# Second MLP product of an attention and MLP kernel: 512 columns of each tile in a PSUM bank of its own, the remaining 128 of all tiles in a fifth bank, finished first

## The chip, the core and the metric

The kernel runs on one core of one Trainium2 chip. The metric is the time of one execution on the device, in microseconds (us); the median of several executions is compared. The core's engines are named as in the profile: PE (TensorE, matrix products into PSUM), PEld (its weight loads), DVE (VectorE), ACT (ScalarE), POOL (GpSimd) and SP (SyncE, which issues most DMAs). All of them run their own instruction streams in order and wait for each other by semaphores.

## What is computed

Two rounds of a sliding-window attention layer and an MLP, on 2048 tokens of 640 channels, in float32:

```python
x = A_x
x = x + attention(layernorm(x), A_wqkv, A_wo)      # 32 heads of 20, 8 keys at distance 2
x = x + mlp(layernorm(x), B_w1, B_b1, B_w2, B_b2)
x = x + attention(layernorm(x), A_wqkv, A_wo)
x = x + mlp(layernorm(x), B_w1, B_b1, B_w2, B_b2)

def mlp(x, w1, b1, w2, b2):
    y = layernorm(x)
    h = gelu(y @ w1 + b1)          # 640 -> 1536
    return h @ w2 + b2             # 1536 -> 640: the second MLP product
```

## The kernel before

**Units and rounds.** The tokens are cut into four units of 512 tokens (four tiles of 128), and there are two rounds, so eight unit-rounds `n` = 0 to 7. Each goes through the product for q, k and v (`qkv`, matmuls at L513), the windowed attention, which is nearly all DVE work (`attention`, L580 to L627), the output product (`project`, matmuls at L646, 120 for a unit, fed by four DMA transposes of `ohl` that SP issues at L635), a layernorm (`layernorm`, L444 to L489) and the MLP (`mlp`, L661). The rounds of different units overlap: while DVE works on the attention of one unit, PE runs the MLP of an earlier one.

**Precision.** Each float32 operand is split into a high and a low float16 half, and a product is three passes (`PASS`, L497): high by high, high by low, low by high. The low half of the hidden values is made on DVE (L694) from the one that ACT makes (L692).

**The MLP.** `PARTS` (L41) gives nine parts: the first unit-round in two parts of two tiles (P0 and P1 here), the others in parts of four tiles (P2 to P8). Each part goes over 12 slices `e` of 128 hidden channels. For each slice PE makes the first product (`inner`, 15 matmuls at L683 into one of three `ps` banks), ACT applies gelu, and PE then adds the slice's share of the second product (`outer`, L699; matmuls at L707) into the tile `accs`, which holds 2560 float32 columns, that is five PSUM banks of 512. Tile `i` of a part holds the columns from `i * 640` to `(i + 1) * 640`, so `outer` cuts it at the bank edges: 512 + 128 columns for tile 0, 384 + 256 for tile 1, 256 + 384 for tile 2, 128 + 512 for tile 3. A slice of a four-tile part is 24 matmuls: four tiles, three passes, two cuts each; in P0 and P1 it is 12. The sums stay in `accs` over all 12 slices. In the last slice, when a tile is finished, DVE adds its 640 columns to the residual stream `xf` (`residual`, L718 to L720), and in the second round SP stores the tile (L725).

**What sets the order.** The order on each engine is not that of the loops. Every step is handed to a planner (`Plan`, L49) with an estimated duration, a priority, what it needs, what it gives and which buffers (`use`) it takes. The planner runs a model of the engines and then emits all steps in the order in which the model starts them. DVE steps with a priority below -200 may start up to `PATIENCE` (L63) late in the model and still be preferred. Each of the five banks of `accs` is a buffer `acc0` to `acc4` that a part takes and gives back. The waits between engines are not made by the planner: a layer below it adds them, from the tiles that each instruction reads and writes, in the order in which they are emitted. `accs` is one tile.

Of the kernel before, what the change touches and what calls it, by code (L numbers as in the profile page):

```python
# [11 lines left out]
OP = mybir.AluOpType  # L12
AX = mybir.AxisListType

S, D, H, DH, W, DIL, F = 2048, 640, 32, 20, 8, 2, 1536
P = 128
KD = D // P
NF = F // P
# [4 lines left out]
WS = 64.0  # L23
EPS = 1e-5
BANK = 512


UNITS = ((0, 0, 4), (0, 512, 4), (1, 0, 4), (1, 512, 4))
NU = len(UNITS)
M = 4  # L30
# [18 lines left out]
class Plan:  # L49
# [10 lines left out]
    REACH = 1.2  # L60
    LAND = 1.0

    PATIENCE = 0.7  # L63
    ORDERED = ("qk", "v", "yT", "o", "ohl", "c1", "c2", "hh", "h32", "ev")

    def __init__(self, slots):
# [9 lines left out]
    def add(self, eng, dur, prio, emit, need=(), give=(), use=(), table=None, move=0.0, lazy=False):  # L76
        o = dict(eng=eng, dur=dur, prio=prio, emit=emit, need=need, give=give, use=use, table=table,
                 move=move, lazy=lazy, n=len(self.ops))
        self.ops.append(o)
        for u in use:  # L80
            if u not in self.users and u[0] in self.ORDERED and u not in self.line.setdefault(u[0], []):
                self.line[u[0]].append(u)
            self.users[u] = self.users.get(u, 0) + 1
# [107 lines left out]
def sliding_dilated_then_mlp_kernel(  # L191
# [60 lines left out]
    def tile_of(pool, key):  # L252
        return T[pool][plan.slot[pool, key]]
# [31 lines left out]
    def dve(n, prio, emit, need=(), give=(), use=(), more=0.0):  # L285
        plan.add("dve", v_cost(n) + more, prio, emit, need, give, use)
# [11 lines left out]
    def mm(cols, n, prio, emit, need=(), give=(), use=()):  # L298
        plan.add("pe", cols / 2400.0 + 0.0028 * n, prio, emit, need, give, use)
# [117 lines left out]
    def layernorm(n, prio, yk, twice):  # L417
# [25 lines left out]
        for t in range(0 if fast else m):  # L443
            act(D, prio, lambda t=t: nc.scalar.activation(junk, x[u][:, t], AF.Copy, scale=-1.0 / D,  # L444
                                                          accum_out=col(0)[:, t:t + 1]),
                need=[("xh", n, t, 0), ("xh", n, t, 1)] if twice else [("x", la, u, t)], give=[("mn", name, t)],
                use=[lk], acc=1)
            act(D, prio, lambda t=t: nc.scalar.activation(junk, x[u][:, t], AF.Square, bias=col(0)[:, t:t + 1],
                                                          accum_out=col(1)[:, t:t + 1]),
                need=[("mn", name, t)], give=[("sq", name, t)], use=[lk], acc=1, ptr=1)  # L450
# [210 lines left out]
    def mlp(at, b, t0, t1):  # L661

        la, u = divmod(b, NU)
        nt = (t1 - t0) * P
        yk = ("yT", ("b", b))
        ready = [("yT", ("b", b), t) for t in range(t0, t1)]

        def banks(i):
            return [(f"acc{k}", at) for k in range(i * D // BANK, ((i + 1) * D - 1) // BANK + 1)]

        for e in range(NF):
            j = at * NF + e
            pk, hk, h32 = ("ps", ("in", j)), ("hh", j), ("h32", j)
            ck, wk = ("c1", j), ("c2", j)
            for i, k in enumerate((ck, wk)):
                dma(328, -250 + j + 1.5 * i, lambda k=k, i=i, e=e: nc.sync.dma_start(tile_of(*k), mw[i][e]),
                    need=[("mw", e, i)], give=[k], use=[k])

            def inner(ck=ck, pk=pk):
                i = 0  # L680
                for k in range(KD):
                    for a, c in PASS:
                        nc.tensor.matmul(tile_of(*pk)[:, :nt], tile_of(*ck)[:, a, k * P:(k + 1) * P],  # L683
                                         transposed(yk)[:, c * KD + k, t0 * P:t1 * P], start=i == 0, stop=i == 3 * KD - 1)
                        i += 1

            mm(3 * KD * nt, 15, j - 1.0 - AHEAD, inner, need=[*ready, ck, *split_done] + [("hhi", j - 2)] * (e > 1), give=[("hp", j)],
               use=[yk, ck, pk])
            act(nt, -430, lambda pk=pk, h32=h32, e=e: nc.scalar.activation(  # L689
                tile_of(*h32)[:, :nt], tile_of(*pk)[:, :nt], AF.Gelu_apprx_tanh, bias=b1[:, e:e + 1], scale=1.0 / WS),  # L690
                need=[("hp", j), "b1"], give=[("h", j)], use=[pk, h32], table="gelu", ptr=1)
            act(nt, -440, lambda h32=h32, hk=hk: nc.scalar.activation(tile_of(*hk)[:, 0, :nt], tile_of(*h32)[:, :nt], AF.Copy),  # L692
                need=[("h", j)], give=[("hhi", j)], use=[h32, hk])
            dve(nt, -1000, lambda h32=h32, hk=hk: nc.vector.tensor_sub(  # L694
                tile_of(*hk)[:, 1, :nt], tile_of(*h32)[:, :nt], tile_of(*hk)[:, 0, :nt]),
                need=[("hhi", j)], give=[("hlo", j)], use=[h32, hk])
            seen = set()

            def outer(i, passes, wk=wk, hk=hk, e=e, seen=seen):  # L699
                cuts = [i * D]  # L700
                while cuts[-1] < (i + 1) * D:
                    cuts.append(min((i + 1) * D, (cuts[-1] // BANK + 1) * BANK))
                for a, c in passes:
                    for c0, c1 in zip(cuts, cuts[1:]):
                        first = e == 0 and c0 // BANK not in seen
                        seen.add(c0 // BANK)
                        nc.tensor.matmul(accs[:, c0:c1], tile_of(*hk)[:, a, (i - t0) * P:(i - t0 + 1) * P],  # L707
                                         tile_of(*wk)[:, c, c0 - i * D:c1 - i * D], start=first,
                                         stop=e == NF - 1 and (a, c) == PASS[-1], skip_group_check=True)

            for i in range(t0, t1):
                prev = [("out", b, e - 1, i)] if e else ([("outh", b, e, i - 1)] if i > t0 else [])
                mm(2 * D, 4, j, lambda i=i, outer=outer: outer(i, PASS[:2]), need=[("hhi", j), wk, *prev],
                   give=[("outh", b, e, i)], use=[wk, hk, *banks(i)])
                mm(D, 2, j - 0.1, lambda i=i, outer=outer: outer(i, PASS[2:]), need=[("hlo", j), ("outh", b, e, i)],
                   give=[("out", b, e, i)], use=[wk, hk, *banks(i)])
        for i in range(t0, t1):
            def residual(i=i):  # L718
                xt = x[u][:, i]
                nc.vector.scalar_tensor_tensor(xt, accs[:, i * D:(i + 1) * D], 1.0 / WS, xt, op0=OP.mult, op1=OP.add)  # L720

            dve(D, -990, residual, need=[("out", b, NF - 1, i), ("xb", b, i)], give=[("x", la + 1, u, i)],
                use=banks(i))
            if la == 1:
                dma(328, -900, lambda i=i: nc.sync.dma_start(rows(out, u)[:, i], x[u][:, i]),  # L725
                    need=[("x", la + 1, u, i)], give=[("done", u, i)])


    load_x(0, -1000)
# [59 lines left out]
```

## Time and profile before

| | us |
|---|---|
| Median of three runs | 1186.52 (1186.27 to 1188.34) |
| The profiled execution | 1188.67 |
| Its span, first to last instruction | 1186.7 |
| PE busy | 1152.7 (97%) |
| DVE busy | 1015.5 (86%) |
| ACT busy | 511.2 (43%) |

An instruction's busy time on PE overlaps the next one's, since matmuls are pipelined: what a matmul costs is the distance from its start to the next one's. The idle time of a group is the time for which its engine stood still just before it, with the instruction that ended the wait. In the timeline, a row can hold several like instructions in succession; its shape is that of the first. Where nothing else is said, times in the trace count from the start of the span.

### The profile page before, as it was taken

The numbers are of one execution on the slowest core, as the hardware profiler recorded it, in microseconds if no ns is written. First come the engines' busy times: TensorE is split into PE (matmuls) and PEld (weight loads), VectorE is DVE, ScalarE is ACT, GpSimd is POOL, SyncE is SP. The second block draws the span as 40 slices with busy tenths as digits, with TensorE's granted clock in tenths as the row PEclk, the third lists the DMA queues.
The fourth block names the chain that finished last, engine by engine and source line by source line (L and its number), as shares of the span: only waits on it lengthen the run. The fifth ranks groups of instructions, "written<-read, shape, count | busy, mean of one in ns | idle before, by whom it ended". The sixth has DMA issues, their size and how long they took to land.

```text
span 1186.7 us, 17119 instructions
## 1 busy us (share of the span) xinstructions
PE 1152.7 (97%) x6844; PEld 643.8 (54%) x6844; DVE 1015.5 (86%) x979; ACT 511.2 (43%) x921; POOL 54.9 (5%) x46
## 2 busy tenths in 40 slices
PE   5999999999999999999999999999999999999997
PEld 2444446577555465445655465556455655565554
DVE  6999999999999999899999999999999999721211
ACT  5476433545265335632626254364333433352111
POOL 1001001100000000200000010010100000000000
PEclk9999999999999999999999999999999999999999
DMA  9999999778876568557556658575856764544431
GB/s 299 278 331 250 306 337 297 226 255 263 210 196 210 177 157 206 163 167 229 133 182 190 196 135 212 172 206 161 191 185 197 186 212 131 138 110 126 137 100 67
DMA packets 219628, 234.99 MB, mean 198 GB/s; under 512 B 129868, under 2 KB 170140, under 8 KB 219548
## 3 DMA queue, kind: packets, MB, share of 16 engines
q1 hardware_dynamic: 190492, 194.57, 58.2%
q10 hardware_dynamic: 29056, 39.33, 10.0%
q8 instruction: 53, 0.87, 0.3%
q14 instruction: 27, 0.22, 0.1%
HBM read 158.93 MB, written 44.78 MB: 172 GB/s over the span
## 4 chain that ended last, share of the span: by engine, by line
PE 88%; DVE 6%; DMA 3%; issue 1%; ACT 1%; POOL 1%; SPq 0%; DVEq 0%; ACTq 0%
PE ps L513 31%; PE accs L707 24%; PE ps L683 23%; PE ps L646 10%; DVE xf L720 1%; DVE pr L580 1%; DVE sm L584 1%; DMA yT<-hl 1%; POOL ln L461 1%; DVE pr L606 1%; DVE pr L614 1%; DMA qk<-spill 1%; DMA c<-mw 1%; DMA pr<-in_A_wqkv_dram 0%; ACT hl L478 0%
## 5 line engine op out<-in xcount | busy, mean ns | idle before, releaser
L513 PE MATMUL ps<-wq,yT 128*128 128x480 f16 x1920 | 392.8, 367 | 2.0 <-DVE wq L344 1.1
L707 PE MATMUL accs<-c,act 128*128 128x512 f16 (+3 forms) x2304 | 333.0, 299 | 16.6 <-DVE xf L720 12.8
L683 PE MATMUL ps<-yT,c 128*128 128x512 f16 (+1 forms) x1620 | 328.2, 356 | 0.6 <-DMA yT<-hl 0.5
L513 PEld LDWEIGHTS <-yT 128*128 128x128 f16 x1920 | 188.0, 98 | 203.7 <-issue 4.7
L707 PEld LDWEIGHTS <-act 128*128 128x128 f16 x2304 | 204.9, 98 | 139.2 <-issue 18.1
L683 PEld LDWEIGHTS <-c 128*128 128x128 f16 x1620 | 158.1, 98 | 146.0 <-issue 0.8
L689 ACT ACTIVATE act<-ps,b 128x512 f32<-128x512 f32 (+1 forms) x108 | 68.9, 638 | 296.0 <-PE ps L683 285.8
L580 DVE TENSOR_TENSOR pr<-qk 128x2560 f32<-128x2560 f32 x64 | 179.2, 2802 | 1.9 <-DMA qk<-spill 1.8
L584 DVE TENSOR_REDUCE sm<-pr 128x128 f32<-128x2560 f32 x64 | 179.5, 2805 | 0.0
L606 DVE TENSOR_TENSOR pr<-sm,v 128x2560 f32<-128x2560 f32 x64 | 179.0, 2817 | 0.1
L694 DVE TENSOR_TENSOR act<-act 128x512 f16<-128x512 f32 (+1 forms) x108 | 67.7, 628 | 102.9 <-ACT act L692 102.2
L519 ACT ACTIVATE ev<-ps 128x480 f32<-128x480 f32 x128 | 72.3, 566 | 168.1 <-PE ps L513 163.2
L614 DVE TENSOR_TENSOR pr<-pr 128x640 f32<-128x640 f32 (+1 forms) x128 | 144.1, 1150 | 0.0
L646 PE MATMUL ps<-wo,yT 128*128 128x320 f16 x960 | 131.8, 299 | 0.0
L646 PEld LDWEIGHTS <-yT 128*128 128x128 f16 x960 | 93.7, 98 | 37.7 <-DMA yT<-ohl 0.4
L461 POOL TENSOR_TENSOR ln<-ln,half 128x2 f32<-128x2 f32 (+1 forms) x30 | 48.4, 1613 | 973.4 <-ACT ln L458 973.4
L444 ACT ACTIVATE junk<-xf 128x640 f16<-128x640 f32 x56 | 41.1, 733 | 82.7 <-DVE xf L652 65.3
L692 ACT ACTIVATE act<-act 128x512 f16<-128x512 f32 (+1 forms) x108 | 62.5, 580 | 2.6
L480 DVE TENSOR_TENSOR hl<-y,hl 128x640 f16<-128x640 f32 x64 | 51.5, 817 | 7.2 <-ACT hl L478 7.2
L478 ACT ACTIVATE hl<-y 128x640 f16<-128x640 f32 x64 | 45.8, 728 | 20.3 <-DMA yT<-hl 14.2
L475 ACT ACTIVATE y<-xf,ln 128x640 f32<-128x640 f32 x56 | 49.5, 908 | 3.6 <-DVE hl L480 3.5
L720 DVE SCALAR_TENSOR_TENSOR xf<-accs,xf 128x640 f32<-128x640 f32 x32 | 25.5, 822 | 26.1 <-PE accs L707 26.1
(51 smaller groups left out, 466.0 us busy)
## 6 DMA issues: line engine op xcount, KB each, us to landing
c<-mw SPq DMA_DIRECT2D x216, 320.0 KB, 3.2
spill<-ev ACTq DMA_DIRECT2D x64, 480.0 KB, 4.6
qk<-spill SPq DMA_DIRECT2D x32, 880.0 KB, 6.6
v<-spill SPq DMA_DIRECT2D x32, 880.0 KB, 4.7
qk<-spill SPq DMA_DIRECT2D x32, 320.0 KB, 3.5
mw<-c ACTq DMA_DIRECT2D x24, 320.0 KB, 6.3
act<-in_B_w_dram SPq DMA_DIRECT2D x21, 320.0 KB, 7.6
xf<-in_A_x_dram SPq DMA_DIRECT2D x16, 320.0 KB, 5.5
```

The lines of the kernel that those rows point to most:

```text
L513: nc.tensor.matmul(ps, transposed(yk)[:, a * KD + k, t * P:(t + 1) * P], wq[:, b, k, g], start=j == 0, stop=j == 3 * KD - 1)
L519: act(3 * GC, -400 + n, lambda i=i, pk=pk, ek=ek: nc.scalar.activation(tile_of(*ek)[:, :, i], tile_of(*pk)[:, :3 * GC].rearrange("p (a c) ...
L580: nc.vector.tensor_mul(tile_of(*pk), w[:, HALO + m + t0:HALO + m + t0 + EH, None, :].to_broadcast([P, EH, W, GC]), windows(w, t0, [GC, W], ...
L584: dve(E, G - 0.7, lambda pk=pk, t0=t0: nc.vector.tensor_reduce(lg(t0, t0 + EH).rearrange("p t w h -> p (t w h)"), tile_of(*pk).rearrange(" ...
L606: nc.vector.tensor_mul(tile_of(*vk).rearrange("p t w (h d) -> p t (w h) d", d=DH), lg(t0, t0 + EH).rearrange("p t w h -> p t (w h)")[:, :, ...
L614: dve(EH * w * GC, G - 0.9, lambda vk=vk, w=w: nc.vector.tensor_add(tile_of(*vk)[:, :, 0:w], tile_of(*vk)[:, :, 0:w], tile_of(*vk)[:, :, w ...
L646: nc.tensor.matmul(tile_of(*pk)[:, :D // 2], transposed(yk)[:, a * KD + k, t * P:(t + 1) * P], wo[:, b, k, c * D // 2:(c + 1) * D // 2], s ...
L683: nc.tensor.matmul(tile_of(*pk)[:, :nt], tile_of(*ck)[:, a, k * P:(k + 1) * P], transposed(yk)[:, c * KD + k, t0 * P:t1 * P], start=i == 0 ...
L689: act(nt, -430, lambda pk=pk, h32=h32, e=e: nc.scalar.activation(tile_of(*h32)[:, :nt], tile_of(*pk)[:, :nt], AF.Gelu_apprx_tanh, bias=b1[ ...
L692: act(nt, -440, lambda h32=h32, hk=hk: nc.scalar.activation(tile_of(*hk)[:, 0, :nt], tile_of(*h32)[:, :nt], AF.Copy), need=[("h", j)], giv ...
L694: dve(nt, -1000, lambda h32=h32, hk=hk: nc.vector.tensor_sub(tile_of(*hk)[:, 1, :nt], tile_of(*h32)[:, :nt], tile_of(*hk)[:, 0, :nt]), nee ...
L707: nc.tensor.matmul(accs[:, c0:c1], tile_of(*hk)[:, a, (i - t0) * P:(i - t0 + 1) * P], tile_of(*wk)[:, c, c0 - i * D:c1 - i * D], start=fir ...
```

## The change

Tile `i` of a part now has its first 512 columns in bank `i`, and its last 128 (the rest, `REST = D - BANK`) in the fifth bank, at `2048 + i * 128`. Each tile has the same two cuts, 512 + 128. In the slices before the last, the order of the steps is that of before. In the last slice the products of the rests come first (high half for all tiles, then low half for all), then tile by tile those of 512 columns. DVE's residual becomes five steps for a four-tile part: one for the rests of all tiles (from one bank, 4 x 128 columns) and one of 512 columns for each tile; in P0 and P1 the step for the rests has 2 x 128 columns. The layernorm and the store of a tile need both of its pieces. `PATIENCE` goes from 0.7 to 0.6.

```diff
 BANK = 512
+REST = D - BANK
...
-    PATIENCE = 0.7
+    PATIENCE = 0.6
...
-                need=[("xh", n, t, 0), ("xh", n, t, 1)] if twice else [("x", la, u, t)], give=[("mn", name, t)],
+                need=[("xh", n, t, 0), ("xh", n, t, 1)] if twice else [("x", la, u, t)] + [("xr", la, u, t)] * la, give=[("mn", name, t)],
...
-        def banks(i):
-            return [(f"acc{k}", at) for k in range(i * D // BANK, ((i + 1) * D - 1) // BANK + 1)]
+        last = ("acc4", at)
+
+        def bank(i):
+            return (f"acc{i}", at)
...
-            def outer(i, passes, wk=wk, hk=hk, e=e, seen=seen):
-                cuts = [i * D]
-                while cuts[-1] < (i + 1) * D:
-                    cuts.append(min((i + 1) * D, (cuts[-1] // BANK + 1) * BANK))
+            def outer(i, passes, parts, wk=wk, hk=hk, e=e, seen=seen):
                 for a, c in passes:
-                    for c0, c1 in zip(cuts, cuts[1:]):
+                    for part in parts:
+                        c0, c1 = (i * BANK, (i + 1) * BANK) if part == 0 else (M * BANK + i * REST, M * BANK + (i + 1) * REST)
...
+            tiles = range(t0, t1)
+            if e < NF - 1:
...
+                continue
+            prev = [("out", b, e - 1, i) for i in tiles]
+            mm(2 * REST * len(tiles), 2 * len(tiles), j, lambda outer=outer: [outer(i, PASS[:2], (1,)) for i in tiles],
+               need=[("hhi", j), wk, *prev], give=[("outh", b, e, ("rest", at))], use=[wk, hk, last])
+            mm(REST * len(tiles), len(tiles), j - 0.2, lambda outer=outer: [outer(i, PASS[2:], (1,)) for i in tiles],
+               need=[("hlo", j), ("outh", b, e, ("rest", at))], give=[("out", b, e, ("rest", at))], use=[wk, hk, last])
+            for i in tiles:
+                mm(2 * BANK, 2, j, lambda i=i, outer=outer: outer(i, PASS[:2], (0,)), need=[("hhi", j), wk, *prev],
+                   give=[("outh", b, e, i)], use=[wk, hk, bank(i)])
+                mm(BANK, 1, j - 0.1, lambda i=i, outer=outer: outer(i, PASS[2:], (0,)), need=[("hlo", j), ("outh", b, e, i)],
+                   give=[("out", b, e, i)], use=[wk, hk, bank(i)])
+
+        def add(xs, ps):
+            nc.vector.scalar_tensor_tensor(xs, ps, 1.0 / WS, xs, op0=OP.mult, op1=OP.add)
+
+        dve(REST * (t1 - t0), -991, lambda: add(
+            x[u][:, t0:t1, BANK:], accs[:, M * BANK + t0 * REST:M * BANK + t1 * REST].rearrange("p (t c) -> p t c", c=REST)),
+            need=[("out", b, NF - 1, ("rest", at)), *[("xb", b, i) for i in range(t0, t1)]], give=[("xr", la + 1, u, i) for i in range(t0, t1)],
+            use=[last])
         for i in range(t0, t1):
...
-            dve(D, -990, residual, need=[("out", b, NF - 1, i), ("xb", b, i)], give=[("x", la + 1, u, i)],
-                use=banks(i))
+            dve(BANK, -990, lambda i=i: add(x[u][:, i, :BANK], accs[:, i * BANK:(i + 1) * BANK]),
+                need=[("out", b, NF - 1, i), ("xb", b, i)], give=[("x", la + 1, u, i)], use=[bank(i)])
```

**Where the order moves.** Three places, in the order of the built programs; a name in brackets is the semaphore of the engine that the instruction waits for (`DVE_49` is DVE's, `PE_49` PE's), and LDWEIGHTS rows are PE's weight loads.

The first is PE in the last slice of P8, the kernel's last part. Before, four of the six matmuls of tile 1:

```order
L707 MATMUL accs<-c_83,act 128x256
L707 LDWEIGHTS act
L707 MATMUL accs<-c_83,act 128x384
L707 LDWEIGHTS act
L707 MATMUL accs<-c_83,act 128x256
L707 LDWEIGHTS act
L707 MATMUL accs<-c_83,act 128x384 [waits DVE_49]
```

Now, the three matmuls into bank 0 and the three into bank 1, behind the twelve for the rests (the line is L709 now):

```order
L709 MATMUL accs<-c_83,act 128x512
L709 LDWEIGHTS act
L709 MATMUL accs<-c_83,act 128x512
L709 LDWEIGHTS act
L709 MATMUL accs<-c_83,act 128x512 [waits DVE_49]
L709 LDWEIGHTS act
L709 MATMUL accs<-c_83,act 128x512
L709 LDWEIGHTS act
L709 MATMUL accs<-c_83,act 128x512
L709 LDWEIGHTS act
L709 MATMUL accs<-c_83,act 128x512 [waits DVE_49]
```

In both programs such a wait is for a residual step of the same part, which stands earlier in the emitted order. All matmuls into `accs` that wait for DVE number 21 before and 26 now. Eight of each are the first matmul of the next part; the other 13 and 18 stand inside a last slice, by part P0 to P8: 1, 1, 2, 1, 0, 1, 2, 2, 3 before, and 0, 2, 4, 0, 1, 3, 2, 2, 4 now.

The second is DVE at the same place. Before, with the residuals of P8 at the end (the fourth one stands in a row of its own behind these):

```order
L694 TENSOR_TENSOR act<-act 128x512 [waits DVE_49,PE_49,Activation_49] x2
L489 TENSOR_TENSOR xf<-xf,b_101 128x640
L694 TENSOR_TENSOR act<-act 128x512 [waits DVE_49,PE_49,Activation_49] x2
L489 TENSOR_TENSOR xf<-xf,b_101 128x640
L694 TENSOR_TENSOR act<-act 128x512 [waits DVE_49,PE_49,Activation_49] x3
L720 SCALAR_TENSOR_TENSOR xf<-accs,xf 128x640 [waits PE_49] x3
```

Now:

```order
L698 TENSOR_TENSOR act<-act 128x512 [waits DVE_49,PE_49,Activation_49] x2
L490 TENSOR_TENSOR xf<-xf,b_101 128x640
L698 TENSOR_TENSOR act<-act 128x512 [waits DVE_49,PE_49,Activation_49] x2
L490 TENSOR_TENSOR xf<-xf,b_101 128x640
L698 TENSOR_TENSOR act<-act 128x512 [waits DVE_49,PE_49,Activation_49] x3
L734 SCALAR_TENSOR_TENSOR xf<-accs,xf 128x4x128 [waits DVE_49,PE_49]
L734 SCALAR_TENSOR_TENSOR xf<-accs,xf 128x512 [waits PE_49] x4
```

Each of the residual steps waits for PE, and in P8 there are five of them where there were four.

The third is PE behind the first product of the sixth slice of P5. Before, 75 matmuls of the product for q, k and v of the last unit-round follow, and then the output product of unit-round 5:

```order
L683 MATMUL ps_95<-yT_73,c_80 128x512
L683 LDWEIGHTS c_80
L683 MATMUL ps_95<-yT_73,c_80 128x512
L513 LDWEIGHTS yT_72
L513 MATMUL ps_96<-wq,yT_72 128x480
```

Now the output product comes at once, and the 75 matmuls behind it:

```order
L687 MATMUL ps_95<-yT_73,c_80 128x512
L687 LDWEIGHTS c_80
L687 MATMUL ps_95<-yT_73,c_80 128x512
L647 LDWEIGHTS yT_74
L647 MATMUL ps_96<-wo,yT_74 128x320
```

The output products of unit-rounds 6 and 7 also stand further forward than before, that of 6 now between the matmuls of P5's eleventh slice instead of P6's second, that of 7 in P7's third slice instead of behind its fourth. The number of matmuls and of their columns is the same in all.

## Rows read from the trace of the kernel before

**Rows 1.** The page: busy time of PE and of DVE, share of the span.

```profile
PE 1152.7 (97%) x6844; PEld 643.8 (54%) x6844; DVE 1015.5 (86%) x979; ACT 511.2 (43%) x921; POOL 54.9 (5%) x46
```

**Rows 2.** Waits of PE: who for whom, us in total, times, longest us.

```profile
PE accs L707 <- DVE xf L720: 12.8, 13, 1.8
PE accs L707 <- DVE act L694: 2.2, 1, 2.2
PE accs L707 <- DMA c<-mw: 1.5, 2, 1.3
PE ps L683 <- DMA yT<-hl: 0.5, 1, 0.5
```

**Rows 3.** Timeline of PE at P5's end: start, us, what [idle before, releaser].

```profile
910.43 3.15 PE L707 MATMUL accs<-c,act 128*128 128x512 f16 x22
914.49 0.43 PE L707 MATMUL accs<-c,act 128*128 128x128 f16 x2 [0.91 <-DVE xf L720]
```

**Rows 4.** Timeline of DVE at P5's end.

```profile
913.62 0.82 DVE L720 SCALAR_TENSOR_TENSOR xf<-accs,xf 128x640 f32<-128x640 f32 x1 [0.80 <-PE accs L707]
914.96 0.82 DVE L720 SCALAR_TENSOR_TENSOR xf<-accs,xf 128x640 f32<-128x640 f32 x1 [0.52 <-PE accs L707]
```

**Rows 5.** Chain of waits, 850 to 870 us: start, us, what.

```profile
858.61 3.26 PE accs L707 x24
861.87 3.24 PE ps L683 x15
```

**Rows 6.** Timeline of PE at P2's end.

```profile
477.32 1.52 PE L707 MATMUL accs<-c,act 128*128 128x512 f16 x10
480.69 1.79 PE L707 MATMUL accs<-c,act 128*128 128x384 f16 x12 [1.84 <-DVE xf L720]
```

**Rows 7.** Timeline of DVE at P2's end.

```profile
478.41 1.49 DVE L614 TENSOR_TENSOR pr<-pr 128x1280 f32<-128x1280 f32 x1
479.81 0.82 DVE L720 SCALAR_TENSOR_TENSOR xf<-accs,xf 128x640 f32<-128x640 f32 x1
```

**Rows 8.** Groups by line: engine, tiles, count, busy us, mean ns, idle before.

```profile
L646 PE MATMUL ps<-wo,yT 128*128 128x320 f16 x960 | 131.8, 299 | 0.0
L652 DVE SCALAR_TENSOR_TENSOR xf<-ps,xf 128x320 f32<-128x320 f32 x64 | 30.3, 486 | 15.8 <-PE ps L646 14.7
L720 DVE SCALAR_TENSOR_TENSOR xf<-accs,xf 128x640 f32<-128x640 f32 x32 | 25.5, 822 | 26.1 <-PE accs L707 26.1
```

**Rows 9.** Timeline of PE early on: five 128-column matmuls with their own weights.

```profile
18.07 0.44 PE L398 MATMUL accs<-ident,hl 128*128 128x128 f16 x5
```

**Rows 10.** Timeline of DVE behind P4's end: four residuals in succession.

```profile
770.99 3.02 DVE L720 SCALAR_TENSOR_TENSOR xf<-accs,xf 128x640 f32<-128x640 f32 x4
```

**Rows 11.** Timeline of PE behind P4's end.

```profile
770.79 3.40 PE L683 MATMUL ps<-yT,c 128*128 128x512 f16 x15
774.06 3.42 PE L707 MATMUL accs<-c,act 128*128 128x512 f16 x24
```

**Rows 12.** Timeline of PE at P1's end.

```profile
352.18 1.52 PE L707 MATMUL accs<-c,act 128*128 128x256 f16 x10 [1.34 <-DMA c<-mw]
354.61 0.43 PE L707 MATMUL accs<-c,act 128*128 128x128 f16 x2 [0.92 <-DVE xf L720]
355.54 1.67 PE L683 MATMUL ps<-yT,c 128*128 128x512 f16 x7 [0.49 <-DMA yT<-hl]
```

**Rows 13.** Timeline of PE around the output product of unit-round 5.

```profile
793.55 15.35 PE L513 MATMUL ps<-wq,yT 128*128 128x480 f16 x75
808.74 4.51 PE L646 MATMUL ps<-wo,yT 128*128 128x320 f16 x32
```

**Rows 14.** Timeline of SP there: the transposes that feed this product.

```profile
800.17 7.57 SPq L635 DMA_TRANSPOSE yT<-ohl  x4
```

**Rows 15.** DMA issues: count, median us from issue to landing.

```profile
yT<-ohl SPq DMA_TRANSPOSE x32, 5.0
```

More of the change, by code (lines that the diff above doesn't have):

```diff
@@ L707, in outer @@
                         nc.tensor.matmul(accs[:, c0:c1], tile_of(*hk)[:, a, (i - t0) * P:(i - t0 + 1) * P],
-                                         tile_of(*wk)[:, c, c0 - i * D:c1 - i * D], start=first,
+                                         tile_of(*wk)[:, c, part * BANK:part * BANK + c1 - c0], start=first,
                                          stop=e == NF - 1 and (a, c) == PASS[-1], skip_group_check=True)
[L711 to L716, printed above, removed]
@@ L717, in mlp @@
-        for i in range(t0, t1):
-            def residual(i=i):
-                xt = x[u][:, i]
-                nc.vector.scalar_tensor_tensor(xt, accs[:, i * D:(i + 1) * D], 1.0 / WS, xt, op0=OP.mult, op1=OP.add)
-            dve(D, -990, residual, need=[("out", b, NF - 1, i), ("xb", b, i)], give=[("x", la + 1, u, i)],
-                use=banks(i))
+            tiles = range(t0, t1)
+            if e < NF - 1:
+                for i in tiles:
+                    prev = [("out", b, e - 1, i)] if e else ([("outh", b, e, i - 1)] if i > t0 else [])
+                    mm(2 * D, 4, j, lambda i=i, outer=outer: outer(i, PASS[:2], (0, 1)), need=[("hhi", j), wk, *prev],
+                       give=[("outh", b, e, i)], use=[wk, hk, bank(i), last])
+                    mm(D, 2, j - 0.1, lambda i=i, outer=outer: outer(i, PASS[2:], (0, 1)), need=[("hlo", j), ("outh", b, e, i)],
+                       give=[("out", b, e, i)], use=[wk, hk, bank(i), last])
+                continue
@@ new lines, in mlp @@
+            for i in tiles:
+                mm(2 * BANK, 2, j, lambda i=i, outer=outer: outer(i, PASS[:2], (0,)), need=[("hhi", j), wk, *prev],
[4 more added lines that the diff above has]
+            nc.vector.scalar_tensor_tensor(xs, ps, 1.0 / WS, xs, op0=OP.mult, op1=OP.add)
@@ L724, in mlp @@
             if la == 1:
                 dma(328, -900, lambda i=i: nc.sync.dma_start(rows(out, u)[:, i], x[u][:, i]),
-                    need=[("x", la + 1, u, i)], give=[("done", u, i)])
+                    need=[("x", la + 1, u, i), ("xr", la + 1, u, i)], give=[("done", u, i)])
     load_x(0, -1000)
```

## The prediction

> **What bounds the kernel now.** I read the page first: PE is busy for 97% of the span and DVE for 86% [rows 1]. So the question is what the few idle microseconds of PE are, and the list of PE's waits answers it: the largest by far, 12.8 us in 13 pieces, is the second MLP product (L707) waiting for DVE's residual steps (L720); behind 200 us all others together are under 5 us [rows 2]. Since PE is the bound and nothing else stops it for long, a microsecond that PE loses or regains inside the kernel is one at its end, unless PE then meets a later wait.
>
> The timeline of one such place shows what a wait is. At P5's end PE issues 22 of the 24 matmuls of the last slice, stops, and goes on 0.91 us later [rows 3]. DVE's first residual step started right as the 22nd matmul ended and had itself waited 0.80 us for PE [rows 4]. That step reads tile 0, whose six matmuls had ended long before (columns 0 to 639, banks 0 and 1); the matmul that waits for it writes tile 3's columns from 1920, in bank 3. So neither wait is about data or a bank. The two engines take turns over the whole tile `accs`: a residual step that stands between two matmuls in the emitted order waits for the one and holds the other.
>
> **The price of one turn.** A slice of 24 matmuls takes 3.26 us, so a pair of cuts (640 columns) 0.272 us [rows 5]. 22 matmuls from 910.43 are through at 913.42; the next started at 914.49 [rows 3]. One turn costs 1.07 us: 0.82 of DVE work [rows 4] and 0.25 of handing over and refilling PE. Before there were 13 turns: 13.9 us. At one of them DVE came late, since a 1.49 us attention step stood ahead of the residual [rows 7], and PE waited 1.84 us instead of 0.92 [rows 6]: 0.9 more, 14.8 us in all.
>
> **The change, part by part.**
>
> *The turns.* The change gives each tile's large piece a bank of its own, but `accs` stays one tile, and the built order still has matmuls of the last slice that wait for DVE: 18 now, 13 before. A step from PSUM takes 0.486 us for 320 columns and 0.822 for 640 [rows 8]; on that line 512 columns take 0.69 and 256 take 0.42. I assume the same for the rests, whose 4 x 128 columns lie together in PSUM and apart in `xf`; no row has this shape, and twice the line's slope for them would add some 0.3 us a turn for six turns, 2 us. So a turn costs 0.69 + 0.25 = 0.94 us, and 0.67 us for the one step of 256 columns that is a turn (P1). Now: 17 x 0.94 + 0.67 = 16.7 us. Lateness of DVE comes on top: before, 0.9 us over 13 turns, so an estimate of 1.3 us for 18, with 0 and 4 us as ends (four times the observed, since one step ahead of a residual lasts up to 2.8 us and only its tail can be late). Together 18.0, against 14.8: **+3.2 us**.
>
> *The matmuls.* Their number and columns stay the same. The twelve rests in succession are each 128 columns with their own weight load. Five like that, early on, took 0.44 us with the last one's tail [rows 9], some 0.055 us each as columns alone would ask, so weights don't bind: 0.
>
> *The next part's first matmul.* Where all residuals stand behind the last matmul, the next part's product waits for the last of them; between them PE has one first product, 3.24 us [rows 5]. After P4 four steps of 640 columns took 3.02 us [rows 10] and PE went on at once [rows 11]. After P3 there are now five of up to 512: 0.14 us shorter each, so about 4 x 0.60 + 0.69 = 3.1 us, with 0.25 of handing over: **+0.1 us**.
>
> *P1.* PE loses 0.5 us more here (0.67 + 0.94 against 1.07), but right behind it PE waits 0.49 us for a transpose [rows 12], and that wait takes it up: **-0.5 us**. The 1.34 us on weights stays.
>
> *The end.* Behind the last matmul the residual has 512 columns instead of 640: **-0.1 us**.
>
> *The moved products and `PATIENCE`.* The planner's new order puts the output products of unit-rounds 5 to 7 further forward. Each is released by attention on DVE and a transpose. Unit-round 5's was issued at 800.17 [rows 14] and lands after 5.0 us [rows 15], the product started at 808.74 behind 75 matmuls of 15.2 us [rows 13]: a margin of 3.6 us. Without these 75 ahead, and with DVE as late as before, PE would wait 15.2 - 3.6 = 11.6 us, and the later two would find PE already late. With the attention steps brought forward as the planner meant, it is 0. I take 0, because the same planner placed all eight of these products before with 0.0 us of idle time at them [rows 8]; 11.6 is the upper end.
>
> Sum: 3.2 + 0.1 - 0.5 - 0.1 = **+2.7 us**. The profiled execution took 1188.67 us with a span of 1186.7; like for like it would be 1191.4. It is 2.15 us above the median of the runs, 1186.52, and I take the sum onto that median: **1189.2 us**. About 0.2% (2.4 us) is what a measurement of this kernel can tell from no change, so the forecast, slower, lies just beyond that bound.
>
> **A rule against this forecast.** Rows 3 and 4 show PE and DVE waiting for each other on disjoint banks. The Trainium skill, "PSUM — Partial Sum Buffer", section "Summary: rules for kernel authors", says that PSUM may be read while a matmul runs if the two are in different banks, and that semaphores should guard it by bank. By that rule this change frees PE; the waits that the trace shows are coarser than the rule asks.
>
> **The rivals.**
>
> 1. *Waits by bank: faster.* If residuals and matmuls of different banks ran side by side, all 18 turns would go: 14.8 us less and 0.2 at the end, 1171.5 us. It decides if the matmul behind a residual step starts before that step ends. For it: each residual now has a bank that no later matmul of the part touches. Against it: rows 3 and 4, where the banks were disjoint too, and the waits in the built order. 3%.
> 2. *Early waits are regained: slightly faster.* PE's waits of 2.2, 1.5 and 0.5 us around P0 and P1 [rows 2] fall away with the new order, and DVE is never late: 2.7 + 0.5 (no wait left to take up P1's loss) - 1.3 - 4.2 = -2.3, 1184.2 us, right at the bound. For it: they hang on when a DMA and a DVE step come, which any reordering moves. Against it: the order up to P1 is nearly the same. 12%, half of it beyond the bound.
> 3. *No late DVE: no change to be seen.* The turns cost what I count, but the residuals are first in DVE's queue: 2.7 - 1.3 = +1.4, or 1187.9 us, and up to 2.4 more than before. For it: twelve of 13 turns were not late. 30%.
> 4. *PE waits at the moved output products.* At the middle of the bounds, 5.8 us: 1195.0 us; at the end 1200.8. It decides at the first of them that stands further forward than its margin (P5's sixth slice). For it: 15.2 us of lead against 3.6 of margin. Against it: 0.0 idle before. 17%.
>
> **How the numbers follow.** The forecast itself, 1188.9 to 1192, has 38%: it is where 18 turns with some late DVE fall, and the likeliest. With rival 4 that makes 55% slower by over 0.2%; rival 3 and half of rival 2 are the 36% within; rival 1 and the other half the 9% faster. The range leaves out rival 1, most of rival 2 and the upper half of rival 4, and takes in the doubt about the rest's shape and DVE's lateness: 1186.0 to 1195.0; the forecast's own range is 1188 to 1192.
>
> **What the profile will show.** Right: some 18 pieces of idle PE before L709 released by the residual (L734), 0.78 us each (0.94 less the 0.16 by which a matmul's tail hides the gap: 1.07 against 0.91 in rows 3), 14 us or more in all instead of 12.8; residual steps of 0.69 us; 0 at L647. Wrong: fewer than 13 such pieces (rival 1), idle time of microseconds at L647 (rival 4), or a time below 1186.

## The result and the profile after

The change is a little slower: 1189.74 us in the median of 22 runs (1187.54 to 1194.14), against 1186.93 (1183.29 to 1192.13, 22 runs) for the kernel before on the same chip. The ratio is 1.0027, with a 95% interval of 1.0018 to 1.0037. The forecast was 1189.2 us, slower, with a range of 1186.0 to 1195.0.

The page of the change, busy times (engine, us, share of the span of 1187.0 us, instructions); it answers to [rows 1]:

```profile
PE 1154.0 (97%) x6844; PEld 620.6 (52%) x6844; DVE 1015.8 (86%) x988; ACT 514.0 (43%) x923; POOL 47.8 (4%) x46
```

PE's waits in the change (who for whom, us in total, times, longest us), against [rows 2]:

```profile
PE accs L709 <- DVE xf L734: 13.8, 18, 0.8
...
PE accs L709 <- DMA c<-mw: 1.3, 1, 1.3
...
PE accs L709 <- DVE act L698: 0.6, 1, 0.6
```

The bound and the wait are those of before: PE at 97%, and the second MLP product waiting for the residual steps, now in 18 pieces instead of 13. At the end of P8, PE's timeline shows the turns of the new layout:

```profile
1173.72 3.17 PE L709 MATMUL accs<-c,act 128*128 128x512 f16 x28
1177.67 0.81 PE L709 MATMUL accs<-c,act 128*128 128x512 f16 x3 [0.78 <-DVE xf L734]
1179.26 0.81 PE L709 MATMUL accs<-c,act 128*128 128x512 f16 x3 [0.78 <-DVE xf L734]
1180.85 0.81 PE L709 MATMUL accs<-c,act 128*128 128x512 f16 x3 [0.78 <-DVE xf L734]
1182.44 0.38 PE L709 MATMUL accs<-c,act 128*128 128x512 f16 x1 [0.78 <-DVE xf L734]
```

DVE's timeline beside it:

```profile
1176.93 0.69 DVE L734 SCALAR_TENSOR_TENSOR xf<-accs,xf 128x512 f32<-128x512 f32 x1 [5.55 <-PE accs L709]
1178.52 0.69 DVE L734 SCALAR_TENSOR_TENSOR xf<-accs,xf 128x512 f32<-128x512 f32 x1 [0.90 <-PE accs L709]
```

A slice of 7680 columns takes 3.26 us [rows 5], so 512 columns take 0.217 and three such matmuls 0.65; but the starts are 1.59 us apart: 0.94 us lost in each turn. By the built order, a row of three is the third matmul into one bank and the first two into the next. The first DVE row is the step for the rests, the second reads bank 0. That step starts at 1178.52, when the second matmul into bank 1 has ended, though the last one into bank 0 was two matmuls earlier; and it holds the third matmul into bank 1, which starts at 1179.26. The two engines alternate over banks that differ, as in [rows 3] and [rows 4].

The residual steps and the output product in the groups by line of the change, against [rows 8] (out<-in, shape, count | busy us, mean ns | idle before):

```profile
L647 PE MATMUL ps<-wo,yT 128*128 128x320 f16 x960 | 131.7, 299 | 0.0
...
L734 DVE SCALAR_TENSOR_TENSOR xf<-accs,xf 128x512 f32<-128x512 f32 x39 | 25.7, 688 | 30.4 <-PE accs L709 30.4
```

The 39 steps of 512 columns (32 tiles and the rests of seven four-tile parts) take 0.69 us, and nothing waits at L647.

### The profile page after: what moved, and what is told of

It is laid out like the page before. It is cut to its first block, busy times and chain, and to the rows that moved or that the text cites. A ratio compares the mean times of both kernels' runs of the same rounds, so it can differ in the third digit from the quotient of the medians.

```text
span 1187.0 us, 17118 instructions
## 1 busy us (share of the span) xinstructions
PE 1154.0 (97%) x6844; PEld 620.6 (52%) x6844; DVE 1015.8 (86%) x988; ACT 514.0 (43%) x923; POOL 47.8 (4%) x46
## 4 chain that ended last, share of the span: by engine, by line
PE 93%; DVE 4%; DMA 2%; issue 1%; ACT 0%; SPq 0%; DVEq 0%
PE ps L514 31%; PE accs L709 26%; PE ps L687 25%; PE ps L647 11%; DVE xf L734 1%; DMA c<-mw 1%; DMA pr<-in_A_wqkv_dram 1%; DVE sm L585 1%; DVE pr L581 0%; DVE pr L607 0%; DVE pr L615 0%; PE accs L399 0%; DVE wq L345 0%; SPq L340 0%; DVE hl L481 0%
## 5 line engine op out<-in xcount | busy, mean ns | idle before, releaser
L709 PE MATMUL accs<-c,act 128*128 128x512 f16 (+1 forms) x2304 | 333.9, 299 | 15.8 <-DVE xf L734 13.8
L709 PEld LDWEIGHTS <-act 128*128 128x128 f16 x2304 | 181.1, 98 | 158.0 <-issue 16.5
L687 PEld LDWEIGHTS <-c 128*128 128x128 f16 x1620 | 154.5, 98 | 149.6 <-issue 3.4
L698 DVE TENSOR_TENSOR act<-act 128x512 f16<-128x512 f32 (+1 forms) x108 | 67.5, 627 | 102.9 <-ACT act L696 102.4
L615 DVE TENSOR_TENSOR pr<-pr 128x1280 f32<-128x1280 f32 (+1 forms) x128 | 144.2, 1151 | 0.0
L647 PE MATMUL ps<-wo,yT 128*128 128x320 f16 x960 | 131.7, 299 | 0.0
L647 PEld LDWEIGHTS <-yT 128*128 128x128 f16 x960 | 93.8, 98 | 37.2
L462 POOL TENSOR_TENSOR ln<-ln,half 128x2 f32<-128x2 f32 (+1 forms) x30 | 41.5, 1383 | 968.0 <-ACT ln L459 968.0
L734 DVE SCALAR_TENSOR_TENSOR xf<-accs,xf 128x512 f32<-128x512 f32 (+1 forms) x41 | 26.5, 675 | 31.4 <-PE accs L709 31.4
```

Source lines behind the costliest of these rows:

```text
L615: dve(EH * w * GC, G - 0.9, lambda vk=vk, w=w: nc.vector.tensor_add(tile_of(*vk)[:, :, 0:w], tile_of(*vk)[:, :, 0:w], tile_of(*vk)[:, :, w ...
L647: nc.tensor.matmul(tile_of(*pk)[:, :D // 2], transposed(yk)[:, a * KD + k, t * P:(t + 1) * P], wo[:, b, k, c * D // 2:(c + 1) * D // 2], s ...
L698: dve(nt, -1000, lambda h32=h32, hk=hk: nc.vector.tensor_sub(tile_of(*hk)[:, 1, :nt], tile_of(*h32)[:, :nt], tile_of(*hk)[:, 0, :nt]), nee ...
```

## The experiments

The theory (A in most of the expectations): the turns cost, 18 now and 13 before, and they come from `accs` being one tile. The rival: the new order, by `PATIENCE`, costs. And for both: what is chance in a single profile?

### The two kernels again

The kernel before, profiled a second time:

> The kernel before once more, for its profile alone. If the turns are fixed by the order, the same 13 pieces of idle PE stand before L707 at the same parts, 0.92 us each; the late DVE at P2 (0.9 us more), the 2.2 us at P0 and the 0.5 us at P2's first product are chance if they are gone or elsewhere.

The change, profiled a second time:

> The change again, profile only. If DVE's lateness at the turns is chance, as the second profile of the kernel before suggests (13 pieces of 0.92 us, 11.9 us in all), the 18 pieces are again 13.8 us in all, none above 0.8 us; if the change makes DVE late in some executions, one or more is 1 us or longer. The waits of 0.6 us on DVE (L698) and 1.3 on a DMA near 240 and 350 us may differ by a microsecond or two: they hang on when a transfer and an attention step come.

The kernel before took 1185.65 us this time and the change 1189.44. PE's waits in the second profile of the kernel before:

```profile
PE accs L707 <- DVE xf L720: 11.9, 13, 0.9
...
PE accs L707 <- DMA c<-mw: 1.3, 2, 1.0
```

PE's waits in the second profile of the change:

```profile
PE accs L709 <- DVE xf L734: 13.8, 18, 0.8
...
PE accs L709 <- DVE act L698: 2.8, 2, 2.2
...
PE accs L709 <- DMA c<-mw: 0.5, 1, 0.5
```

| us | before | before again | change | change again |
|---|---|---|---|---|
| span | 1186.7 | 1183.7 | 1187.0 | 1187.5 |
| residual turns, idle | 12.8 | 11.9 | 13.8 | 13.8 |
| the hidden values' low half (L694, L698) | 2.2 | 0 | 0.6 | 2.8 |
| weights by DMA | 1.5 | 1.3 | 1.3 | 0.5 |

The wait of 2.2 us for L694 is there in one profile of each kernel, so it is chance, and so is the late DVE of [rows 6]: 13 pieces are 0.92 us each the second time. The 18 of the change add up to the same 13.8 us in both. With the 0.16 us that a matmul's tail hides in each, the turns cost 11.9 + 13 x 0.16 = 14.0 us before and 13.8 + 18 x 0.16 = 16.7 now. That is +2.7 us; the medians differ by 2.8. The smaller terms, of some tenths each, are taken up with the prediction below.

### Five tiles of one bank each

```diff
-    accs = psum.tile([P, M * D], FT, name="accs")
+    accs = many(psum, 5, [P, BANK], FT, "accs")
...
-                        nc.tensor.matmul(accs[:, c0:c1], tile_of(*hk)[:, a, (i - t0) * P:(i - t0 + 1) * P],
+                        nc.tensor.matmul(accs[c0 // BANK][:, c0 % BANK:c0 % BANK + c1 - c0], tile_of(*hk)[:, a, (i - t0) * P:(i - t0 + 1) * P],
```

In the change, with the residual steps addressed likewise; the order on PE, DVE and SP is the same in both traces:

> The changed kernel with accs as five tiles of one bank each, nothing else; the emitted order is that of the changed kernel, and no matmul of a last slice waits for DVE any more (18 did). Theory A (the 18 turns of 0.94 us come from accs being one tile): no idle PE before the second product inside a last slice; 16.7 us less than the changed kernel, 1173 us, if PE meets no later wait; up to 1181 us if PE, now early, meets the transposes that feed the output products, whose margin in the changed kernel is about 2 us. Theory B (the bank or the engines themselves make PE and DVE alternate): the 18 pieces stay, 1189.7 us.

In the kernel before, where a residual step is cut in two at the bank edge:

> The kernel before with accs as five tiles of one bank each; a tile's residual becomes two steps, one for each bank it lies in. The emitted order of the other steps is that of before. Tiles still share banks, and 8 matmuls of last slices wait for DVE (13 before). Theory A: only the piece in the shared bank is waited for, 128 to 384 columns, 0.53 to 0.80 us a turn: some 5 us instead of 14.8, so about 1177 us, and more if PE then meets a later wait; the layout of the change is worth these 5 us once the waits are by bank. Theory B (alternation whatever the tile): 1186.9 us or more, since there are twice as many residual steps.

The change with five tiles takes 1174.92 us in the median of 4 runs, ratio to before 0.9891 (0.9867 to 0.9914); the kernel before with five tiles 1177.95 in that of 6, ratio 0.9925 (0.9898 to 0.9952). The change with five tiles at P8's end, PE and then DVE:

```profile
1163.79 5.60 PE L709 MATMUL accs<-c,act 128*128 128x512 f16 x40
```

```profile
1166.84 3.28 DVE L734 SCALAR_TENSOR_TENSOR xf<-accs,xf 128x512 f32<-128x512 f32 x5 [5.12 <-PE accs L709]
```

PE runs its matmuls in one piece from 1163.79 to the end at 1169.4; four of DVE's five steps run beside them, and the fifth follows. PE's list of waits has no line for these steps (L734) any more. In the kernel before with five tiles, eight pieces are left, at places where two tiles of a part share a bank; one at P8's end, in PE's timeline, and their line in PE's waits:

```profile
1163.74 3.80 PE L707 MATMUL accs<-c,act 128*128 128x256 f16 x27
1167.92 0.97 PE L707 MATMUL accs<-c,act 128*128 128x384 f16 x6 [0.38 <-DVE xf L723]
```

```profile
PE accs L707 <- DVE xf L723: 4.5, 8, 1.6
```

So the turns came from the one tile: 0.9891 / 1.0027 = 0.9864, 16 us less than the change, for 16.7 us of turns. The interval of so few runs is some 3 us to either side, and the profiled spans differ by 13 (1174.2 against 1187.0 and 1187.5); there PE also meets a few new waits, 1.5 us of them at the output products. That no turn is left is what the profile shows directly. With the tiles apart the new layout also has none of the 4.5 us in eight pieces, since its rests, which share a bank, are all done before; the intervals of the two ratios overlap a little, so the profiles show this, not the times.

### All residual steps behind the part's last matmul

```diff
-            need=[("out", b, NF - 1, ("rest", at)), *[("xb", b, i) for i in range(t0, t1)]], give=[("xr", la + 1, u, i) for i in range(t0, t1)],
+            need=[("out", b, NF - 1, t1 - 1), ("out", b, NF - 1, ("rest", at)), *[("xb", b, i) for i in range(t0, t1)]], give=[("xr", la + 1, u, i) for i in range(t0, t1)],
...
-                need=[("out", b, NF - 1, i), ("xb", b, i)], give=[("x", la + 1, u, i)], use=[bank(i)])
+                need=[("out", b, NF - 1, i), ("out", b, NF - 1, t1 - 1), ("xb", b, i)], give=[("x", la + 1, u, i)], use=[bank(i)])
```

`accs` stays one tile, and no turn is left inside a part.

> The changed kernel with accs still one tile, but every residual step of a part also needs the part's last matmul, so that none stands between two matmuls of a last slice: 0 turns. Theory A: the 16.7 us of turns go; the five steps then all stand behind the last matmul, which costs 0.1 to 0.3 us at each of seven next parts and 4 x 0.60 = 2.4 us behind P8: about 1176 us, up to 1184 if PE meets later waits. Theory C (the turns are not what counts, DVE's time is): no gain, 1189 us or more, since the residuals come later.

1184.21 us, ratio to before 0.9972 (0.9958 to 0.9986). Of the 16.7 us only some 6 came out, less than expected. PE's waits tell part of it:

```profile
PE accs L709 <- DMA c<-mw: 4.6, 1, 4.6
PE accs L709 <- DVE act L698: 2.2, 1, 2.2
PE accs L709 <- DVE xf L734: 1.6, 2, 0.8
```

Two turns went over into P3's first slice. At the end five residual steps (3.08 us) stand behind the last matmul instead of one of 0.69. And at P1's end PE waits 4.6 us for the weights of the last slice, and goes on below full clock; the windows of this profile (stretch, length, busy us of PE, PEld, DVE, ACT and POOL, granted clock, DMA share, GB/s):

```profile
350.00:360.00 10.00, 5.36 (x30) 2.75 (x29) 10.00 (x8) 0.05 (x1) 0.00 (x0) 0.72 1.09 289
```

PE's timeline there:

```profile
356.98 2.93 PE L709 MATMUL accs<-c,act 128*128 128x128 f16 x11 [4.64 <-DMA c<-mw]
359.71 2.64 PE L687 MATMUL ps<-yT,c 128*128 128x512 f16 x8
```

A second profile asks whether that is chance:

> The change with all residual steps behind the last matmul of their part, again, profile only. The first profile had no turn inside a part, but a wait of 4.8 us for weights at 357 us and one of 2.4 us for DVE at 238 us, each followed by 3 to 4 us of matmuls at half clock. If those come from the order (DVE does other steps ahead of the one that is waited for), they recur within a microsecond; if they are chance, they are gone and the span is 1178 to 1181 us.

It took 1185.02 us, and the wait is back (4.4 us, granted clock 0.66 from 350 to 360), so the wait for the weights comes with the order. L698's is back too (2.4 us in two pieces); but one profile of each of the two kernels has one of 2.2 us as well, so that one is not told from chance.

### `PATIENCE` alone, and the layout alone

```diff
-    PATIENCE = 0.7
+    PATIENCE = 0.6
```

In the kernel before:

> The kernel before with PATIENCE 0.6 and nothing else: the output products of the later unit-rounds move, the layout stays, and the built order again has 13 matmuls of a last slice that wait for DVE (0, 1, 1, 2, 2, 2, 0, 2, 3 by part). Theory A (the change is slower by its turns alone, and the moved order costs nothing): 13 turns of 1.08 us as before, so within 1.2 us of before, ratio 0.999 to 1.001; idle time at L646 stays at 0.3 us or less. Theory B (the new PATIENCE and the order that follows from it make the change slower): 2.5 to 3 us more than before, ratio about 1.0025, with waits at L646 or L707 that the kernel before has not.

And 0.7 in the change:

> The change with the old PATIENCE, 0.7: the new layout alone. The built order has 16 turns (2, 2, 2, 0, 1, 2, 1, 2, 4 by part), of which two are for a step of 256 columns. Theory A (turns): 14 x 0.94 + 2 x 0.68 = 14.5 us of turns, against 16.7 in the change and 14.0 before: 2.2 us less than the change and 0.5 more than before, ratio to before 0.9995 to 1.0015. Theory B (PATIENCE): with the old value the loss of the change goes, equal to before or faster. The two agree nearly here; it is the other run that separates them, this one shows whether the number of turns in the new layout counts as computed.

Both were slower than expected: 1191.99 us, ratio 1.0039 (1.0021 to 1.0057), and 1195.17 us, ratio 1.0066 (1.0042 to 1.0089). PE's waits with `PATIENCE` 0.6 in the old layout:

```profile
PE accs L707 <- DVE xf L720: 11.0, 12, 0.9
...
PE accs L707 <- DMA c<-mw: 4.5, 1, 4.5
PE accs L707 <- DVE act L694: 2.3, 2, 1.7
```

And with 0.7 in the new layout:

```profile
PE accs L709 <- DVE xf L734: 12.0, 16, 0.8
...
PE ps L687 <- DMA yT<-hl: 6.1, 1, 6.1
```

The turns are as counted: 16 in the new layout; in the old one 12 of the 13, the one behind the long wait doesn't show. The loss is at P1's end, near 350 us, the same place as in the experiment before, and no wait is at the output products. DVE there, with `PATIENCE` 0.6 in the old layout:

```profile
343.52 0.77 DVE L480 TENSOR_TENSOR hl<-y,hl 128x640 f16<-128x640 f32 x1
344.20 0.42 DVE L694 TENSOR_TENSOR act<-act 128x256 f16<-128x256 f32 x1
...
344.87 2.82 DVE L584 TENSOR_REDUCE sm<-pr 128x128 f32<-128x2560 f32 x1
347.59 0.42 DVE L694 TENSOR_TENSOR act<-act 128x256 f16<-128x256 f32 x1
347.93 0.82 DVE L480 TENSOR_TENSOR hl<-y,hl 128x640 f16<-128x640 f32 x1
```

And SP:

```profile
344.32 3.65 SPq L485 DMA_TRANSPOSE yT<-hl  x1
348.06 0.53 SPq L676 DMA_DIRECT2D c<-mw  x1
348.81 2.70 SPq L485 DMA_TRANSPOSE yT<-hl  x1
```

In the second profile of the kernel before, both steps of this layernorm (L480) stand behind that attention step (L584), and SP had issued the same weights 3.6 us sooner, ahead of both transposes:

```profile
341.48 2.81 DVE L584 TENSOR_REDUCE sm<-pr 128x128 f32<-128x2560 f32 x1
...
344.54 0.82 DVE L480 TENSOR_TENSOR hl<-y,hl 128x640 f16<-128x640 f32 x1
...
345.61 0.81 DVE L480 TENSOR_TENSOR hl<-y,hl 128x640 f16<-128x640 f32 x1
```

```profile
344.42 0.32 SPq L676 DMA_DIRECT2D c<-mw  x1
345.42 5.10 SPq L485 DMA_TRANSPOSE yT<-hl  x2
```

With `PATIENCE` 0.6, DVE makes the first of the two layernorm steps ahead of the attention step. Its transpose can then go at 344.3 us and stands ahead of the weights in SP's order; the issue of this transpose alone takes 3.65 us, and the weights go out behind it. The attention step holds only the second transpose, which stands behind the weights. So what held the weights was a transpose that came early, not one that came late, as the next expectation has it. The two profiles with the residual steps behind show the same: this issue takes 4.10 and 3.12 us there, and the weights go out behind it.

In the run with 0.7 in the new layout PE waits for a transpose instead of the weights. It was issued at 351.14 us, behind its layernorm step (ended at 350.96) and behind the issue of another transpose (ended at 351.05), and landed at 357.49; which of the two made it late was not separated.

### The weights out of that queue

First by another issuer, the one load alone (shown for the kernel before; the same in the other):

```diff
-                dma(328, -250 + j + 1.5 * i, lambda k=k, i=i, e=e: nc.sync.dma_start(tile_of(*k), mw[i][e]),
+                dma(328, -250 + j + 1.5 * i, lambda k=k, i=i, e=e: (nc.gpsimd if (at, e, i) == (1, NF - 1, 1) else nc.sync).dma_start(tile_of(*k), mw[i][e]),
```

> The kernel before with PATIENCE 0.6 and one DMA issue moved: the weights of P1's last slice for the second product are issued by POOL instead of SP; PE, DVE and ACT keep their order. In the run without this edit that issue stood in SP's queue behind the transpose of a layernorm half that DVE made late, went out at 348.06 us and landed when PE had waited 4.5 us, with 4 us of matmuls at half clock behind. Theory A (SP's queue held the weights): POOL issues them when their buffer comes free, near 343.5 us, they land near 350, before or right as PE comes to them, the wait of 4.5 us falls to 1.5 us or less, no half clock behind it; the product behind it may then meet the late transpose (0.5 to 3 us). Time 3 to 6 us less than without the edit, ratio to before 0.999 to 1.002. Theory B (the transfer itself is slow, or the buffer comes free late): the wait stays at 4 to 5 us, ratio 1.003 to 1.006. Theory C (the loss of that run lies elsewhere in the new order): the wait goes and the time stays.

> The change with all residual steps behind the last matmul of their part, and the same one DMA issue moved from SP to POOL. Two profiles of it without this edit had a wait of 4.4 and 4.6 us for these weights at P1's end, and half clock behind it, some 6 to 7 us in all. Theory A: that goes; with 0 turns inside parts the span is 1176 to 1180 us, ratio to before 0.991 to 0.995. Theory B (the residuals behind the last matmul cost what the turns did, in other places): the time stays near 1184, ratio 0.996 to 0.999.

Neither helped: 1193.97 us, ratio 1.0061 (1.0048 to 1.0074), and 1186.17, ratio 0.9999 (0.9985 to 1.0012). POOL issued at once, but the load was slow. The issues from 335 to 362 us in the old layout (KB each, median us to landing):

```profile
c<-mw SPq DMA_DIRECT2D x8, 320.0 KB, 3.8
...
c<-mw POOLq DMA_DIRECT2D x1, 320.0 KB, 10.0
```

Issued at 343.43 us it landed at 353.4, and PE waited 5.4 us. That leaves open whether the queue or full DMA engines made it late, since the issuer was changed too. So the load was exchanged with its neighbour in SP's own queue:

```diff
-    for o in plan.run():
+    steps = plan.run()
+    k = ("c2", 2 * NF - 1)
+    i = next(n for n, o in enumerate(steps) if k in o["give"])
+    last = max(n for n in range(i) if any(u != k and u[0] == "c2" and plan.slot[u] == plan.slot[k] for u in steps[n]["use"]))
+    steps.insert(last + 1, steps.pop(i))
+    for o in steps:
         o["emit"]()
```

> The kernel before with PATIENCE 0.6 and two neighbours in SP's queue exchanged: the load of P1's last weights stands ahead of the transpose instead of behind it; every other order is the same. POOL as the issuer sent this load at 343.4 us and it took 10.0 us to land, so who issues and what is in flight both mattered there; here the queue is SP's as before. Theory A (SP's order held the load): it goes out near 344.5 us instead of 348.1 and lands after 5 to 6.5 us, near 350 to 351, and PE's wait for it falls from 4.5 to 0.5 to 2 us. Theory B (transfers are full in this stretch, and the load lands late whenever it is issued): it lands at 353 us or later and the wait stays at 4 us or more. In both, DVE's late half of a layernorm step is still transposed late; under A the product behind may then wait for that transpose until some 355 us, so the time falls by only 0 to 5 us: ratio to before 0.9995 to 1.004 under A, 1.003 to 1.006 under B.

> The change with all residual steps behind the last matmul of their part, with the same exchange in SP's queue. Under A the wait of 4.4 us for the last weights of P1 falls to 0.5 to 2 us, and the time by 0 to 5 us against the 0.997 of the first run, with a wait for the transpose behind it if less than 3 us are won; under B the wait and the time stay (0.996 to 0.999).

In the old layout with `PATIENCE` 0.6: 1188.87 us, ratio 1.0022 (1.0009 to 1.0035), where it had been 1.0039. PE's waits, its timeline and the window of 10 us there:

```profile
PE ps L683 <- issue: 1.8, 1, 1.8
PE accs L707 <- DMA c<-mw: 1.5, 1, 1.5
```

```profile
349.96 1.52 PE L707 MATMUL accs<-c,act 128*128 128x256 f16 x10 [1.54 <-DMA c<-mw]
353.31 6.63 PE L683 MATMUL ps<-yT,c 128*128 128x512 f16 x30 [1.83 <-issue]
```

```profile
350.00:360.00 10.00, 8.17 (x42) 3.91 (x42) 10.00 (x12) 2.97 (x7) 0.00 (x0) 1.00 0.99 301
```

The load went out at 343.56 us instead of 348.06, the wait fell from 4.5 to 1.5 us, and the clock stayed full (0.66 in this window without the exchange). The product behind now waits 1.8 us; the profile names no releaser, but the second transpose, the one behind the attention step, landed at 353.22, 0.1 us before the product started (356.61 and 356.70 in the other run of this exchange). The span fell by 3.8 us, 1189.6 to 1185.8. So SP's order held the load in this kernel. The intervals of the two ratios overlap, so it is the profiles that show it. In the new layout with the residual steps behind, the wait fell only from 4.4 to 2.7 us, with 1.1 behind it at the next product, and the time stayed (1183.18 us, ratio 0.9971, 0.9957 to 0.9985): issued at 345.82, the load took 7.5 us. The queue is a part of the loss there; the rest, transfers that collide and transposes that come late, was not separated.

## Why the prediction was right, and where it was not

**The turns: right.** 18 turns of 0.94 us, one of them 0.67, were forecast as 16.7 us, and 16.7 were measured, in two profiles alike. The rest's shape, for which there was no row, takes the same 0.69 us as a plain step of 512 columns. (The doubt about it was worked out too small: by [rows 8] twice the slope is 0.54 us more for 512 columns, not 0.3.) Each idle piece is 0.78 us, as said, but for the 0.5 us of the step of 256 columns.

**DVE's lateness: wrong.** It was put at 0.9 us before and 1.3 now. It is 0 in the second profile of before and in both of the change. The step that failed took a late start seen once for a share of all turns. Without it on either side the forecast's own numbers give 16.7 - 13.9 = +2.8 for the turns, not +3.2, and +2.3 in all; the medians say +2.8. So it is partly luck that the sum of +2.7 came within 0.1 us: the 0.4 us for lateness, which was not there, stood in for others that were missing. Rival 3 came near but took the lateness from the new kernel alone, +1.4.

**The small terms.** At L647 0.0, as forecast. At P1, the wait for the transpose [rows 12] is gone in the change, as forecast. The next part's first matmul costs 0.1 us behind P3, as forecast (from 625.48 to 628.82 us, 3.34 against 3.24); but behind P0, where no turn is left either, it costs 0.24 us that the forecast does not have. PE's timeline of the change:

```profile
273.66 1.80 PE L687 MATMUL ps<-yT,c 128*128 128x256 f16 x15
275.54 1.79 PE L709 MATMUL accs<-c,act 128*128 128x512 f16 x12
277.16 1.80 PE L687 MATMUL ps<-yT,c 128*128 128x256 f16 x15
278.80 1.79 PE L709 MATMUL accs<-c,act 128*128 128x512 f16 x12
```

15 first-product matmuls take 1.64 us up to the next row's start in the later pair, 1.88 in the earlier. What is left between the sum and the medians, some tenths, is less than what one chance wait moves (2.2 us at L698), and isn't settled.

**The moved order: right in sum, for a reason that does not hold in general.** The term was taken at 0 because the same planner had placed all eight output products without idle time. At those products no run with the one tile waited more than 0.4 us in all. But the price of an order lay elsewhere, at P1's end, where `PATIENCE` 0.6 in the old layout cost 4.6 us (0.39% of 1186) and 0.7 in the new one 6.1 us of wait. Each half of the change alone is slower than both together (ratios of 1.0039 and 1.0066 against 1.0027), so their prices do not add up. The change itself has 1.3 and 0.5 us there, so its order doesn't pay. The prediction named this place only as one where early waits may be regained; that they can grow to 6 us was not priced.

**The rivals.** Rival 1, waits by bank, is the mechanism that would have been there with five tiles: 1171.5 us was its time (0.9873 of before), and 1174.92 (0.9891) was measured when the tiles were apart. In the change itself no turn went; what stood in the way was the tile. The Trainium skill, "PSUM — Partial Sum Buffer", section "Summary: rules for kernel authors", says that PSUM may be read while a matmul runs if the two are in different banks. The run with five tiles agrees: four residual steps of 0.69 us run beside 5.60 us of matmuls that do not stop. Rival 2, early waits regained, is the noise of the table above. Rival 4, microseconds of wait from the moved order, came true at the output products in no run with the one tile; in the runs with one half of the change alone, waits of that size stood at P1's end.

## What to carry to other kernels

Before a layout is changed to free an engine, look at what the waits go by: here they went by the tile, and a layout by banks inside one tile of five banks added turns, while five tiles with the same order gave 1.1% against before. Count such turns in the built order and price one from the starts in the timeline; that gave the change to within half a microsecond. A constant of a planner is a change of its own: try it alone, and look at every engine's queue: one DMA issue of 3.65 us that came to stand ahead of a load cost PE 3 us of wait, and a lower clock behind it.

## What the hardware showed beyond that

PE's granted clock fell behind long waits. In all five profiles in which PE waited 4.4 us or more for the weights at P1's end, the window from 350 to 360 us has 0.66 to 0.72, and 0.70 in the one with a wait of 2.7 us; where the same wait was 1.5 us or less it stayed at 1.00. Behind the wait of 6.1 us for a transpose, in the run with 0.7 in the new layout, it has 0.85, and 0.98 from 360 to 370; only the last 2.3 us of the first window lie behind that wait. The eleven matmuls behind the wait at 356.98 (six of 128 columns, five of 512) take 2.73 us up to the next row's start. At full clock, by 3.26 us for twelve times 640 columns [rows 5], their 3328 columns take 1.41: they ran at the lower level, 1.2 GHz instead of 2.4. A wait of 2.2 us near 237 us was followed by a clock of 1.00 in two profiles (before, change again) and of 0.92, from 230 to 240 us, in a third (residual steps behind). So a long wait cost more than itself, 1.3 us more in these eleven matmuls alone.

The same load of 320 KB took 10.0 and 9.6 us when POOL issued it, and 5.3 to 7.5 us from SP in the same stretch in nine profiles; the share of the DMA engines is 0.84 to 1.15 in all windows of 10 us there (340 to 360). Why POOL's took longer was not separated.
